# A decode step of sliding-window attention plus a gated MLP: the last chunk of w_down in 64 partitions, as eight loads of eight rows

## The chip, the core and the metric

The kernel runs on one core of a Trainium2 chip. A core has TensorE (PE, with its weight loads shown as PEld), VectorE (DVE), ScalarE (ACT), GpSimd (POOL) and SyncE (SP), which issues all the transfers of this kernel; 16 DMA engines carry them. Each engine runs its own list of instructions in order and waits on semaphores. The metric is the device time of one execution in microseconds (us); the time before is the median of three runs.

## The reference

One token for each of two batch rows goes through attention over the last 2048 positions of a cache and, beside it, through a bilinear gated MLP; both results are added to the input.

```python
xn = _layernorm(x, axis=-1)                       # x: [2, 1, 512]
q = (xn @ wq)                                     # 32 heads of 128
k, v = k_cache[:, :, Sk - W:], v_cache[:, :, Sk - W:]   # W = 2048
p = softmax(einsum("bhqd,bhkd->bhqk", q, k) * Dh ** -0.5)
attn = einsum("bhqk,bhkd->bhqd", p, v) @ wo
h = (xn @ w_gate) * (xn @ w_up)                   # F = 1376
out = x + attn + h @ w_down
```

Everything is float32. The two caches alone are 32 heads x 2 x 2048 x 128 values each, so nearly all of the 159 MB that the core reads is read once and used once.

## The kernel before

**Data.** The host lays all inputs out in one long array, `stream`, in the order of use. `blocks()` lists its pieces: for each piece a slot of SBUF, a first column and the fields in it. A field is a kind and an index: `k` and `vp` are a head's keys and values, `wo` and `wq` weights of the attention, `wg` and `wu` the gate and up weights, `wd` a chunk of 128 rows of w_down. Three slots (`step0` to `step2`) of 128 partitions x 15360 columns are used in turn; the small piece that comes first has a tile of its own, `first`, with the transposed input, two constant matrices and the query weights of the first two heads (`AHEAD` is 2, `DH` 128).

**The loads.** `pump()` takes the pieces in order and writes one load for each as soon as no live field lies in its columns; `done()` ends a field's life and calls `pump()` again. All loads go through SP's list, and so in order. The last piece is cut at row `LOW_ROWS` (88) into two loads of 88 and 40 rows.

**How waits come about.** `Flow.add` notes for each operation which operations it depends on: it compares the box of partitions and columns of each tile it touches with the boxes noted earlier. `Flow.box` gives a slice of partitions with a step as the whole stretch from its first to its last partition. `Flow.emit` turns a dependency into a semaphore wait where the two operations have different keys; each load is a key of its own, and any other operation has its engine as key:

```python
p1 = p0 + ps // row * (pn - 1) + 1
if (write or w) and a0 < p1 and p0 < a1 and b0 < f1 and f0 < b1:
    deps.add((m, w))
key = ("dma", n) if make[0] == "dma_start" else unit
```

The first line is from `box`; the next two are from `add` (`w` and `write` say whether the earlier and the later access write); the last is from `emit`.

**The work.** For each head DVE multiplies the keys by the query (`products`) and sums the products (`sums`), POOL and ACT make the softmax, PE multiplies by the values (`weigh`) and, for a group of heads, by `wo`. `gate()` makes the hidden vector of the MLP and transposes it in pieces of 128 into `hT` (and its last 96 values into `hX`); `down(c)` multiplies chunk c of w_down by it. There are ten whole chunks (`NFC` is 10). Chunks 0 and 1 and the rest rows are used early, chunk 2 (`HOLE`) late, and chunks 3 to 9 at the very end. All add up in one PSUM tile, `acc`; near the end each result is spread over four groups of 32 partitions, so that a chunk takes four products with 128 columns each (`accumulate`). In the trace a product in float32 is two matmul records. Chunk 8 comes in two halves by columns (`wh`): one with chunk 7, one with chunk 9 in the last piece. Behind chunk 9 DVE adds the input (`o_out`), and SP stores the result.

Of the kernel before, what the change touches and what calls it, by code (L numbers as in the profile page):

```python
# [15 lines left out]
P = 128  # L16
B, D, H, DH, SK, F = 2, 512, 32, 128, 8192, 1376
# [3 lines left out]
NC = D // P  # L21
FB = 4 * P
NFB = -(-F // FB)
NFC = F // P
FR = F - NFC * P
FH = [(0, 2 * FB), (2 * FB, F)]
RB = 8
M = RB * (B - 1) + 1
# [7 lines left out]
AHEAD = H + 1 - G * T  # L36
GC = G * DH
CQ = NC * GC
FIRST = AHEAD * DH
# [4 lines left out]
NE = 2  # L44
HOLE = NE
TAIL = list(range(NE + 1, NE + 5))
LOW_ROWS = 88
STEP = 30 * FB
BUFS = 3
BASE = 30 * 1024  # L50
# [10 lines left out]
def pitch(fields):  # L61

    n = -(-sum(w for _, _, w in fields) // BLK)
    return (n | 1) * BLK


def blocks():

    def k(*heads):
        return [("k", h, CK) for h in heads]

    def vp(h, p0=0, p1=NV):
        return [("vp", (h, p0, p1), FB * (p1 - p0))] + ([("wo", h, CO)] if p1 == NV else [])  # L80

    def wd(chunks):
        return [("wd", c, D) for c in chunks]

    def wh(c, half):
        return [("wh", (c, half), D // 2)]

    gu = [
        (kind, half, NC * (FH[half][1] - FH[half][0])) for half in range(2) for kind in ("wg", "wu")
    ]  # L90
    ones = [("pick", 0, 4 * SIDES * B), ("rows", 0, NFB * B)]
    out = [(None, 0, [("x", 0, B * NC)] + ones + [("w", 0, NC * FIRST)])]
    out.append((1, 0, k(*range(2)) + [("wq", 0, CQ)] + k(*range(2, AHEAD))))
    out.append((2, 0, gu + [("wr", 0, NS * P)] + wd(range(NE))))
    k0, v0 = AHEAD, 0
    for t in range(T - 1):
        a = vp(v0) + vp(v0 + 1, 0, VA)
        b = vp(v0 + 1, VA) + vp(v0 + 2, 0, VB)
        c = vp(v0 + 2, VB) + vp(v0 + 3) + vp(v0 + 4)
        out.append((0, 0, k(k0, k0 + 1) + a))  # L100
        out.append((1, 0, k(k0 + 2, k0 + 3) + [("wq", t + 1, CQ)] + b))
        out.append((2, 0, k(k0 + 4) + c))
        k0, v0 = k0 + G, v0 + G

    def put(slot, at, *groups):
        for fields in groups:
            out.append((slot, at, fields))
            at += sum(w for _, _, w in fields)
        return at

    put(0, 0, k(k0, k0 + 1), vp(v0) + vp(v0 + 1, 0, VA))
    at = put(1, 0, k(k0 + 2) + vp(v0 + 1, VA))
    put(1, at, vp(v0 + 2), k(k0 + 3))
    at = put(2, 0, vp(v0 + 3, 0, VA), vp(v0 + 3, VA), vp(v0 + 4))
    v30, v31 = vp(v0 + 5), vp(v0 + 6)
    put(2, at, v30[:1])
    c = NFC - 2
    put(
        0, 0, v31[:1], v30[1:] + v31[1:] + wd(TAIL[:1]), wd(TAIL[1:]), wd([c - 1]) + wh(c, 0),
        wh(c, 1) + wd([c + 1]),  # L120
    )
    return out


class Flow:
# [296 lines left out]
def sliding_attention_plus_glu_kernel(  # L422
# [6 lines left out]
    flow = Flow(nc)  # L429
    pe, dve, act, pl, sp = (flow.engine(unit) for unit in ("pe", "dve", "act", "pl", "sp"))  # L430
# [6 lines left out]
    first = None  # L437


    todo, at = [], 0  # L440
# [3 lines left out]
    got, live = {}, {}  # L444

    def pump():
        nonlocal first
        while todo:
            slot, c0, fields, at = todo[0]
            c1 = c0 + sum(w for _, _, w in fields)  # L450
            if any(s == slot and a < c1 and c0 < b for s, a, b in live.values()):
                return
            todo.pop(0)
            if slot is None:
                tile = first = flow.tile([P, c1], "first")
            else:
                tile = slots[slot]
            a = c0
            for kind, i, w in fields:
                got[kind, i] = tile[:, a : a + w]  # L460
                if slot is not None:
                    live[kind, i] = (slot, a, a + w)
                a += w
            src = stream[at : at + P * pitch(fields)].rearrange("(p i) -> p i", p=P)
            rows = [0, P] if todo else [0, LOW_ROWS, P]
            for p0, p1 in zip(rows, rows[1:]):
                sp.dma_start(tile[p0:p1, c0:c1], src[p0:p1, : c1 - c0])

    def done(kind, i):
        got.pop((kind, i))  # L470
        live.pop((kind, i), None)
        pump()
# [4 lines left out]
    rows = got["rows", 0]  # L477
# [39 lines left out]
    tr = flow.bank([P, 4 * P], "tr")  # L517
# [20 lines left out]
    xnb = flow.tile([P, NC * B, PB], "xnb")  # L538
# [3 lines left out]
    xnb = xnb.rearrange("p (c b) n -> p c (b n)", b=B)  # L542
# [3 lines left out]
    q_first = tr[:, P : P + FIRST]  # L546
    q_use = flow.bank([P, 2 * FB], "q_use")

    def project_first():
        w = got["w", 0].rearrange("p (c n) -> p c n", c=NC)  # L550
        for c in range(NC):
            pe.matmul(q_first, xnb[:, c, :], w[:, c, :], start=(c == 0), stop=(c == NC - 1))
        got.pop(("w", 0))

    def project_q(t):
        w = got["wq", t].rearrange("p (c n) -> p c n", c=NC)
# [65 lines left out]
    def columns(t):  # L622
        return [t[:, c : c + P] for c in range(0, t.shape[1], P)]

    def accumulate(lhsT, rhs, last=False):
        nonlocal n_acc
        for g in range(4):
            pe.matmul(
                acc_g[32 * g : 32 * g + M, :], lhsT, rhs[g],
                start=(n_acc == 0), stop=last,  # L630
            )
        n_acc += 1
# [54 lines left out]
    hT = flow.tile([P, 4, NFB, M], "hT")  # L687
    dve.memset(hT, 0.0)

    hX = flow.tile([P, NS, M], "hX")  # L690
    dve.memset(hX, 0.0)

# [14 lines left out]
    def gate():  # L707
        g_sb = flow.ring([P, FB], "o_sb", 2)
        act.copy(g_sb, gu_ps[0])
        h_sb = flow.ring([P, FB], "o_sb", 2)  # L710
        dve.tensor_tensor(h_sb, g_sb, gu_ps[1], op=ALU.mult)
        for i in range(4):
            t = tr[:, P + i * P // 2 : P + i * P // 2 + NFB * B]
            pe.matmul(t, h_sb[:, i * P : (i + 1) * P], rows, start=True, stop=True)
            act.copy(hT[:, i, :, ::RB], t.rearrange("p (n b) -> p n b", b=B))
        for i in range(NS):
            t = tr[:, P + (2 * i + 1) * P // 4 : P + (2 * i + 1) * P // 4 + NFB * B]
            f = (NFC % 4) * P + i * FX - FR
            pe.matmul(t, h_sb[:, f : f + P], rows, start=True, stop=True)
            act.copy(hX[FR:, i, ::RB], t[FR:, (NFB - 1) * B :])  # L720

    def down(c):
        lhsT = hT[:, c % 4, c // 4, :]
        if c == HOLE:
            w = got["wq", T - 1].rearrange("p (c n) -> p c n", c=NC)[:, :, GC - DH :]
            pe.matmul(acc, lhsT, w, start=False, stop=False)
            done("wq", T - 1)
        elif c < NE:
            pe.matmul(acc, lhsT, got["wd", c], start=(c == 0), stop=False)
            done("wd", c)  # L730
        else:
            fields = [("wd", c)] if ("wd", c) in got else [("wh", (c, half)) for half in range(2)]
            accumulate(lhsT, sum([columns(got[f]) for f in fields], []), last=(c == NFC - 1))
            for f in fields:
                done(*f)

    def down_rest():
        wr = got["wr", 0]
# [77 lines left out]
    for t in range(T - 1):  # L816
        h = AHEAD + G * t
# [7 lines left out]
    h = H - 4  # L825
    v = G * (T - 1)
    spare, o_ps2 = q_ps[:, :FB], q_ps[:, FB:]
    pair, tile = [v, v + 1], o_ps[0]
# [17 lines left out]
    pair, tile = [v + 2, v + 3], o_ps[1]  # L846
# [24 lines left out]
    for n in (v + 4, v + 5):  # L871
        tile = o_ps[n % 2]
# [14 lines left out]
    n = v + 6  # L887
# [3 lines left out]
    for k, t in enumerate((o_ps[n % 2], o_ps2)):  # L891
        for j in range(NV):
            kk, i = divmod(j, 4)
# [22 lines left out]
def laid_out(x):  # L916
# [4 lines left out]
    first = {  # L921
        kind: np.zeros((P, w), a.dtype) for kind, _, w in blocks()[0][2][:3]
    }
# [13 lines left out]
    wq = x["A_wq"].reshape(P, NC, H * DH)  # L937
# [5 lines left out]
    wd = x["B_w_down"]  # L943
    rest = wd[NFC * P :].reshape(FR, NS + 1, P)

    def field(kind, i):
        if kind in first:
            return first[kind]
        if kind == "k":
            return cache["k"][i]  # L950
        if kind == "vp":
            h, p0, p1 = i
            return cache["v"][h][:, FB * p0 : FB * p1]
        if kind == "w":
            return wq[:, :, :FIRST].reshape(P, -1)
        if kind == "wq":
            h = AHEAD + G * i
            w = wq[:, :, h * DH : (h + G) * DH]
            if i == T - 1:
                hole = wd[HOLE * P : (HOLE + 1) * P].reshape(P, NC, DH)  # L960
                w = np.concatenate([w, hole], axis=2)
            return w.reshape(P, -1)
        if kind == "wo":
            return wo[i]
        if kind == "wr":
            last = rest[:, NS, :].reshape(NS, FX, P).swapaxes(0, 1)
            return np.concatenate([rest[:, :NS, :], last]).reshape(P, NS * P)
        if kind == "wd":
            return wd[i * P : (i + 1) * P]
        if kind == "wh":  # L970
            c, half = i
            return wd[c * P : (c + 1) * P, half * (D // 2) : (half + 1) * (D // 2)]
        return gu[kind][:, :, FH[i][0] : FH[i][1]].reshape(P, -1)

    def part(fields):
# [42 lines left out]
```

## Time and profile before

| | us |
|---|---|
| median of three runs (377.70 to 377.87) | 377.84 |
| the profiled execution, its own time | 377.76 |
| span of its instructions | 376.4 |
| DVE busy | 302.8 |
| PE busy | 213.5 |
| ACT busy | 60.3 |
| POOL busy | 25.7 |

The core's queue of loads moved 159.54 MB in 4807 packets. In the profile all instructions that the helper `Flow` writes stand under one line, L350, so they are told apart by the names of their tiles. A row of the timeline gives the start, the duration, the engine, the operation with what it writes and reads, and in brackets how long the engine sat idle before it and what ended that; "SPq" is the time in which SP issues a transfer, not the transfer. Times of the trace are counted from the start of the span.

### The profile page before, as it was taken

The numbers are of one execution on the slowest core, as the hardware profiler recorded it, in microseconds if no ns is written. First come the engines' busy times: TensorE is split into PE (matmuls) and PEld (weight loads), VectorE is DVE, ScalarE is ACT, GpSimd is POOL, SyncE is SP. The second block draws the span as 40 slices with busy tenths as digits, with TensorE's granted clock in tenths as the row PEclk, the third lists the DMA queues.
The fourth block names the chain that finished last, engine by engine and source line by source line (L and its number), as shares of the span: only waits on it lengthen the run. The fifth ranks groups of instructions, "written<-read, shape, count | busy, mean of one in ns | idle before, by whom it ended". The sixth has DMA issues, their size and how long they took to land. (4 is left out here: it accounts for less than half of the span.)

```text
span 376.4 us, 2737 instructions
## 1 busy us (share of the span) xinstructions
PE 213.5 (57%) x990; PEld 75.5 (20%) x990; DVE 302.8 (80%) x182; ACT 60.3 (16%) x251; POOL 25.7 (7%) x84
## 2 busy tenths in 40 slices
PE   0552957385733285831395650596450677484796
PEld 0321223022200032200131210231110232021243
DVE  2159959999929999839999569999389999999920
ACT  1003120121311121301111301211201212211220
POOL 1000000000000000000000000000000000000000
PEclk9958786959878568968578967588976598889799
DMA  9999999999999999999999999999999999999995
GB/s 384 410 439 442 413 419 444 464 431 437 418 418 424 477 431 444 418 418 418 437 464 431 444 418 418 424 477 431 444 418 418 418 428 429 441 422 421 441 414 177
DMA packets 4813, 159.63 MB, mean 424 GB/s; under 512 B 567, under 2 KB 711, under 8 KB 1351
## 3 DMA queue, kind: packets, MB, share of 16 engines
q1 hardware_dynamic: 4807, 159.54, 98.4%
q8 instruction: 4, 0.07, 0.1%
q14 instruction: 2, 0.02, 0.0%
HBM read 159.48 MB, written 0.07 MB: 424 GB/s over the span
## 5 line engine op out<-in xcount | busy, mean ns | idle before, releaser
L350 PE MATMUL o_ps<-step,p 128*16 128x512 f32 (+3 forms) x512 | 101.3, 797 | 114.7 <-PEq L342 101.9
L350 DVE TENSOR_TENSOR step<-step,q_use 128x4096 f32<-128x4096 f32 x29 | 127.7, 4404 | 32.5 <-DMA step<-in_stream_dram 32.5
L350 DVE TENSOR_REDUCE s<-step 128x32 f32<-128x4096 f32 x32 | 141.4, 4420 | 1.1
L350 PEld LDWEIGHTS o_ps<-step,p 128*16 128x16 f32 (+2 forms) x512 | 21.0, 120 | 180.4 <-issue 161.7
L350 ACT ACTIVATE nm<-mm 128x2 f32<-128x2 f32 x32 | 6.5, 203 | 237.0 <-POOL mm L350 237.0
L350 PE MATMUL acc<-step,oT 128*9 128x512 f32 (+1 forms) x82 | 36.5, 609 | 7.0 <-PEq L342 6.0
L350 PE MATMUL q<-step,xnb 128*128 128x512 f32 (+1 forms) x96 | 30.5, 475 | 6.7 <-PEq L342 6.7
L350 POOL PARTITION_ALL_REDUCE mm<-m x32 | 11.3, 354 | 293.8 <-DVE m L350 293.8
L350 PE MATMUL tr<-first,o_sb 128*128 128x4 f32 (+2 forms) x134 | 23.2, 292 | 13.8 <-PEq L342 13.8
L350 PEld LDWEIGHTS tr<-first,o_sb 128*128 128x128 f32 x134 | 22.3, 244 | 29.8 <-issue 28.1
L350 DVE TENSOR_TENSOR step<-step,tr 128x4096 f32<-128x4096 f32 x3 | 13.2, 4414 | 11.2 <-DMA step<-in_stream_dram 11.2
L350 PEld LDWEIGHTS q<-step,xnb 128*128 128x128 f32 x96 | 16.3, 207 | 24.6 <-issue 24.6
L350 ACT ACTIVATE p<-s,nm 64x32 f32<-64x32 f32 x64 | 20.4, 319 | 1.4
L350 PE MATMUL o_ps<-step,xn 128*2 128x512 f32 (+1 forms) x48 | 12.5, 660 | 7.1 <-PEq L342 7.1
L350 POOL PARTITION_ALL_REDUCE sum<-rs x32 | 12.8, 399 | 39.5 <-ACT p L350 39.5
L350 ACT ACTIVATE oT<-tr,rec 128x1 f32<-128x1 f32 x58 | 10.1, 265 | 18.6 <-PE tr L350 18.6
L350 DVE TENSOR_REDUCE m<-s 64x1 f32<-64x32 f32 x64 | 11.5, 180 | 1.5
L350 ACT COPY o_sb<-o_ps 128x512 f32<-128x512 f32 (+1 forms) x16 | 9.1, 572 | 21.9 <-PE o_ps L350 21.8
L350 ACT ACTIVATION_READ_ACCUMULATOR p<-s,nm 64x1 f32 x64 | 11.8, 185 | 0.0
L350 PEld LDWEIGHTS acc<-step,oT 128*9 128x9 f32 x82 | 5.5, 96 | 24.0 <-issue 21.2
L350 DVE TENSOR_TENSOR oT<-tr,rec 128x2 f32<-128x2 f32 x3 | 0.5, 162 | 10.8 <-PE tr L350 10.8
L350 PE MATMUL acc<-step,hT 128*9 128x128 f32 (+2 forms) x64 | 7.5, 337 | 1.0 <-DMA step<-in_stream_dram 1.0
(47 smaller groups left out, 47.6 us busy)
## 6 DMA issues: line engine op xcount, KB each, us to landing
step<-in_stream_dram SPq DMA_DIRECT2D x15, 7680.0 KB, 35.4
step<-in_stream_dram SPq DMA_DIRECT2D x1, 7424.0 KB, 21.8
step<-in_stream_dram SPq DMA_DIRECT2D x1, 6208.0 KB, 36.0
step<-in_stream_dram SPq DMA_DIRECT2D x3, 2048.0 KB, 34.9
step<-in_stream_dram SPq DMA_DIRECT2D x2, 2304.0 KB, 24.1
step<-in_stream_dram SPq DMA_DIRECT2D x1, 4096.0 KB, 27.6
step<-in_stream_dram SPq DMA_DIRECT2D x1, 3584.0 KB, 28.9
step<-in_stream_dram SPq DMA_DIRECT2D x1, 3072.0 KB, 24.9
```

Source lines behind the costliest of these rows:

```text
L350: made = getattr(eng, method)(*args, **kwargs)
```

## The change

The 64 low and the 64 high rows of chunk 9 now lie side by side in 64 partitions, 1024 columns wide (a field of the new kind `wl`; the stream holds zeros for the other 64 partitions, and these are not loaded). This field is the last piece. It comes as eight loads: for each half of 32 partitions, four loads of eight rows, each with a step of four partitions, so that row number e of each load lies in partition p0 + 4e. Chunks 7 and 8 come whole in the piece before. Chunk 9 then takes eight products over 64 partitions where it took four over 128: four with the low half of its piece of `hT`, four with the high half, which `gate()` transposes once more into a new tile `hL`, at partitions 0 to 63. DVE clears `hL` once. The first piece of the stream becomes two: the input, the constants and the weights of one query head (550 columns), then the weights of the other head (1024 columns), both in the tile `first`.

```diff
-    def wh(c, half):
-        return [("wh", (c, half), D // 2)]
...
-    out = [(None, 0, [("x", 0, B * NC)] + ones + [("w", 0, NC * FIRST)])]
+    fields = [("x", 0, B * NC)] + ones + [("w", 0, NC * DH)]
+    out = [(None, 0, fields)]
+    out.append((None, sum(w for _, _, w in fields), [("w", 1, NC * (FIRST - DH))]))
...
-        0, 0, v31[:1], v30[1:] + v31[1:] + wd(TAIL[:1]), wd(TAIL[1:]), wd([c - 1]) + wh(c, 0),
-        wh(c, 1) + wd([c + 1]),
+        0, 0, v31[:1], v30[1:] + v31[1:] + wd(TAIL[:1]), wd(TAIL[1:]), wd([c - 2, c - 1]),
+        [("wl", c, 2 * D)],
...
-            src = stream[at : at + P * pitch(fields)].rearrange("(p i) -> p i", p=P)
-            rows = [0, P] if todo else [0, LOW_ROWS, P]
-            for p0, p1 in zip(rows, rows[1:]):
-                sp.dma_start(tile[p0:p1, c0:c1], src[p0:p1, : c1 - c0])
+            src = stream[at : at + P * pitch(fields)].rearrange("(p i) -> p i", p=P)[:, : c1 - c0]
+            if fields[0][0] == "wl":
+                for half in range(0, HALF, HALF // 2):
+                    for p0 in range(half, half + 4):
+                        rows = slice(p0, half + HALF // 2, 4)
+                        sp.dma_start(tile[rows, c0:c1], src[rows])
+            else:
+                sp.dma_start(tile[:, c0:c1], src)
...
+    hL = flow.tile([P, M], "hL")
+    dve.memset(hL, 0.0)
...
+        c = NFC - 1
+        t = tr[:HALF, P + 7 * P // 4 : P + 7 * P // 4 + NFB * B]
+        f = c % 4 * P + HALF
+        pe.matmul(t, h_sb[:, f : f + HALF], rows, start=True, stop=True)
+        act.copy(hL[:HALF, ::RB], t[:, c // 4 * B : (c // 4 + 1) * B])
...
+        elif c == NFC - 1:
+            w = columns(got["wl", c][:HALF])
+            accumulate(lhsT[:HALF], w[:4])
+            accumulate(hL[:HALF], w[4:], last=True)
+            done("wl", c)
         else:
-            fields = [("wd", c)] if ("wd", c) in got else [("wh", (c, half)) for half in range(2)]
-            accumulate(lhsT, sum([columns(got[f]) for f in fields], []), last=(c == NFC - 1))
-            for f in fields:
-                done(*f)
+            accumulate(lhsT, columns(got["wd", c]))
+            done("wd", c)
```

The two places where lists of instructions change most are SP's and PE's ends. The rows below name a load by its target and its shape (partitions x columns); `step_49` is slot 0. A name like `done_dma823` is the semaphore of one load. SP's list before, from the load that ends the values of the last heads on:

```order
L350 DMA step_49<-in_stream_dram 128x1536 [waits done_dve]
L350 DMA step_49<-in_stream_dram 128x1536
L350 DMA step_49<-in_stream_dram 128x768
L350 DMA step_49<-in_stream_dram 88x768 [waits done_pe]
L350 DMA step_49<-in_stream_dram 40x768
L350 DMA out_dram<-o_out 128x128 [waits done_dve]
```

The 88 and the 40 rows are the last piece; the second of the two is issued without a wait. SP's list with the change, the same place:

```order
L352 DMA step_49<-in_stream_dram 128x1536 [waits done_dve]
L352 DMA step_49<-in_stream_dram 128x1536
L352 DMA step_49<-in_stream_dram 128x1024
L352 DMA step_49<-in_stream_dram 8x1024 [waits done_pe]
L352 DMA step_49<-in_stream_dram 8x1024 [waits done_dma823]
L352 DMA step_49<-in_stream_dram 8x1024 [waits done_dma824]
L352 DMA step_49<-in_stream_dram 8x1024 [waits done_dma825]
L352 DMA step_49<-in_stream_dram 8x1024
L352 DMA step_49<-in_stream_dram 8x1024 [waits done_dma827]
L352 DMA step_49<-in_stream_dram 8x1024 [waits done_dma828]
L352 DMA step_49<-in_stream_dram 8x1024 [waits done_dma829]
L352 DMA out_dram<-o_out 128x128 [waits done_dve]
```

The eight loads have the semaphores `done_dma823` to `done_dma830`, in order. The second, third and fourth and the sixth, seventh and eighth each stand behind a wait for the load just ahead of them; the fifth has none of its own. PE's list before, from the first chunk of TAIL behind the last head on (`hT` are hidden values, `oT` a head's output):

```order
L350 MATMUL acc<-step_49,hT 9x128 [waits done_dma817]
L350 MATMUL acc<-step_49,hT 9x128 x11
L350 MATMUL acc<-step_49,oT 9x128 [waits done_dve]
L350 MATMUL acc<-step_49,oT 9x128 x3
L350 MATMUL acc<-step_49,hT 9x128 [waits done_dma818]
L350 MATMUL acc<-step_49,hT 9x128 x5
L350 MATMUL acc<-step_49,hT 9x128 [waits done_dma819,done_dma820]
L350 MATMUL acc<-step_49,hT 9x128 x5
```

Six products stand behind the wait for the last piece. PE's list with the change:

```order
L352 MATMUL acc<-step_49,hT 9x128 [waits done_dma821]
L352 MATMUL acc<-step_49,hT 9x128 x11
L352 MATMUL acc<-step_49,oT 9x128 [waits done_dve]
L352 MATMUL acc<-step_49,oT 9x128 x3
L352 MATMUL acc<-step_49,hT 9x128 [waits done_dma822]
L352 MATMUL acc<-step_49,hT 9x128 x7
L352 MATMUL acc<-step_49,hT 9x128 [waits done_dma826,done_dma830]
L352 MATMUL acc<-step_49,hT 9x128 x3
L352 MATMUL acc<-step_49,hL 9x128 x4
```

Eight products now stand behind the last piece, and their one wait is for the fourth and the eighth of the eight loads.

More of the change, by code (lines that the diff above doesn't have):

```diff
@@ L46 @@
 TAIL = list(range(NE + 1, NE + 5))
-LOW_ROWS = 88
+HALF = P // 2
 STEP = 30 * FB
@@ L116, in blocks @@
     put(2, at, v30[:1])
-    c = NFC - 2
+    c = NFC - 1
     put(
-        0, 0, v31[:1], v30[1:] + v31[1:] + wd(TAIL[:1]), wd(TAIL[1:]), wd([c - 1]) + wh(c, 0),
-        wh(c, 1) + wd([c + 1]),
+        0, 0, v31[:1], v30[1:] + v31[1:] + wd(TAIL[:1]), wd(TAIL[1:]), wd([c - 2, c - 1]),
+        [("wl", c, 2 * D)],
     )
     return out
+PRELUDE = sum(w for slot, _, fields in blocks() if slot is None for _, _, w in fields)
 class Flow:
@@ L454, in pump @@
             if slot is None:
-                tile = first = flow.tile([P, c1], "first")
+                first = first or flow.tile([P, PRELUDE], "first")
+                tile = first
             else:
@@ L549, in project_first @@
     def project_first():
-        w = got["w", 0].rearrange("p (c n) -> p c n", c=NC)
+        w = first[:, PRELUDE - NC * FIRST :].rearrange("p (h c n) -> p h c n", h=AHEAD, c=NC)
         for c in range(NC):
-            pe.matmul(q_first, xnb[:, c, :], w[:, c, :], start=(c == 0), stop=(c == NC - 1))
-        got.pop(("w", 0))
+            pe.matmul(
+                q_first.rearrange("p (h n) -> p h n", h=AHEAD), xnb[:, c, :], w[:, :, c, :],
+                start=(c == 0), stop=(c == NC - 1),
+            )
+        for n in range(2):
+            got.pop(("w", n))
     def project_q(t):
@@ L715, in gate @@
             act.copy(hT[:, i, :, ::RB], t.rearrange("p (n b) -> p n b", b=B))
+        c = NFC - 1
+        t = tr[:HALF, P + 7 * P // 4 : P + 7 * P // 4 + NFB * B]
+        f = c % 4 * P + HALF
+        pe.matmul(t, h_sb[:, f : f + HALF], rows, start=True, stop=True)
+        act.copy(hL[:HALF, ::RB], t[:, c // 4 * B : (c // 4 + 1) * B])
         for i in range(NS):
@@ L954, in field @@
         if kind == "w":
-            return wq[:, :, :FIRST].reshape(P, -1)
+            heads = slice(0, 1) if i == 0 else slice(1, AHEAD)
+            w = wq.reshape(P, NC, H, DH)[:, :, heads]
+            return w.transpose(0, 2, 1, 3).reshape(P, -1)
         if kind == "wq":
@@ L969, in field @@
             return wd[i * P : (i + 1) * P]
-        if kind == "wh":
-            c, half = i
-            return wd[c * P : (c + 1) * P, half * (D // 2) : (half + 1) * (D // 2)]
+        if kind == "wl":
+            w = wd[i * P : (i + 1) * P].reshape(2, HALF, D).swapaxes(0, 1).reshape(HALF, -1)
+            return np.concatenate([w, np.zeros_like(w)])
         return gu[kind][:, :, FH[i][0] : FH[i][1]].reshape(P, -1)
```

## The prediction

> **What bounds the kernel now.** First the page's slices, its row on the queue and its chain.
>
> ```profile
> DVE  2159959999929999839999569999389999999920
> DMA  9999999999999999999999999999999999999995
> q1 hardware_dynamic: 4807, 159.54, 98.4%
> HBM read 159.48 MB, written 0.07 MB: 424 GB/s over the span
> DVE 17%; DMA 16%; PE 1%; issue 0%; SPq 0%
> ```
>
> The 16 DMA engines are at nine tenths or more in all slices but the last; no other engine is. DVE comes near it in the middle but has slices at 3 and 2 where it waits for loads. So the time is that of the stream of loads, and what follows the last load. The chain of waits, read from its end, says the same:
>
> ```profile
> 339.54 0.33 SPq L350
> 339.91 32.29 DMA step<-in_stream_dram
> 372.20 0.04 issue
> 372.25 2.23 PE acc L350 x56
> 374.47 0.02 issue
> 374.49 0.29 DVE o_out L350
> ```
>
> The piece that ends late was issued at 339.54 us and landed 32 us later, as it stood behind the stream that had been issued before it. Loads that are issued early thus cost only their bytes. The timeline shows the end in detail:
>
> ```profile
> 343.92 2.18 SPq L350 DMA_DIRECT2D step<-in_stream_dram  x1
> 372.25 0.84 PE L350 MATMUL acc<-step,hT 128*9 128x128 f32 x24 [1.03 <-DMA step<-in_stream_dram]
> 373.27 1.17 PE L350 MATMUL acc<-step,hT 128*9 128x128 f32 x24
> 373.83 0.32 PEld L350 LDWEIGHTS acc<-step,hT 128*9 128x9 f32 x12 [0.24 <-DMA step<-in_stream_dram]
> 374.49 0.29 DVE L350 TENSOR_TENSOR o_out<-acc,x_nat 128x128 f32<-128x128 f32 x1 [3.08 <-PE acc L350]
> 374.81 0.37 SPq L350 DMA_DIRECT2D out_dram<-o_out  x1
> ```
>
> SP had issued the last piece by some 346 us. It landed just ahead of 373.83, where PE starts its last 12 records (six products); these end at 373.27 + 1.17 = 374.44. DVE and the store follow. So the last landing sets the end, at 373.8, and 376.4 - 373.8 = 2.6 us follow it.
>
> **The change part by part.** *The eight loads.* Only the first is issued early: it waits for a product of PE, as the 88-row load did, and goes out from about 344 us on. SP's list in the part on the change shows that the second, third, fourth, sixth, seventh and eighth each wait until the load ahead has landed. The boxes explain it: rows p0, p0+4, ... p0+28 count as one stretch of 29 partitions, so the four loads of a half overlap by the kernel's own bookkeeping though they write different rows. The fifth (partitions 32 on) has no wait, but stands behind the fourth in SP's list. So the loads no longer queue up 25 us ahead; six round trips stand one behind the other: second, third, fourth with the fifth just behind it, sixth, seventh, eighth. Only the wait of SP is new on the path; behind it in SP's list there is only the store, which had to come last anyhow, and PE's last eight products wait for the eighth load.
>
> What one round trip costs, no row shows for a small load in an empty queue. The nearest rows are the store, which meets an empty queue, and the first load of the program:
>
> ```profile
> first<-in_stream_dram SPq DMA_DIRECT2D x1, 787.0 KB, 4.5
> out_dram<-o_out SPq DMA_DIRECT2D x1, 64.0 KB, 1.6
> 7.41 0.54 SPq L350 DMA_DIRECT2D carry<-in_carry_dram  x1
> ```
>
> The store takes 1.6 us from issue to landing. The first load takes 4.5 us, of which 787 KB at 424 GB/s are 1.9, so 2.6 us without its data. A load of 32 KB lies between: 1.4 (a little below the store, which moves twice the bytes) to 2.3 us (below the 2.6, as that one met a program just starting). I take 1.6, by the nearer row, plus 0.03 for SP to see the landing, as the store starts at 374.81 and DVE ended at 374.78. Six trips are 6 x 1.63 = 9.8 us. The fifth load goes out after the fourth has been issued, which took 0.54 us for the small load `carry`; the sixth waits for the fifth, so 0.5 us is added: 10.3 us from the landing of the first load to that of the eighth (6 x 1.43 + 0.5 = 9.1 to 6 x 2.33 + 0.5 = 14.5 at the bounds).
>
> When the first small load lands: the stream holds the same bytes up to the end (128 x 1536 columns before, 128 x 1024 and 64 x 1024 now). In the old tail these ended at 373.8. Seven of eight rows of an engine are not yet issued, 7 x 4 KB; an engine moves 424 / 16 = 26.5 GB/s, so that is 1.1 us less: 372.7. Against this, the end of the stream ran far below its rate:
>
> ```profile
> 368.00:370.00 2.00, 2.00 (x48) 1.15 (x41) 0.00 (x0) 0.51 (x2) 0.00 (x0) 1.00 1.03 413
> 370.00:372.00 2.00, 1.22 (x18) 0.97 (x8) 0.16 (x1) 0.23 (x1) 0.00 (x0) 1.00 0.64 140
> 372.00:374.00 2.00, 1.75 (x52) 1.25 (x54) 0.00 (x0) 0.00 (x0) 0.00 (x0) 1.00 0.10 36
> ```
>
> (The last two columns of this view by stretches are the engines' busy share and GB/s.) From 368 to 370 a busy engine moved 413 / 1.03 / 16 = 25 GB/s, from 370 to 372 only 140 / 0.64 / 16 = 13.7, while the loads of 88 and 40 rows ran. If that slowness came from these two loads, it is gone, and up to 1 us of the 2 us stretch with it. I take 372.0, with 371.3 and 372.7 as bounds. The eighth load then lands at 372.0 + 10.3 = 382.3, against 373.8: 8.5 us later.
>
> The Trainium skill, "DMA: Bandwidth & Descriptors", section "Anatomy of one DMA", speaks against small loads in a chain: each has a fixed cost of about 2.0 us on GpSimd's path, nearly all of it the confirmation that the last byte has landed. No run here shows that path; the store's 1.6 us agrees in kind. By 2.0 us the chain would be an estimated 6 x 2.03 + 0.5 = 12.7 us, and the time 2.4 us longer than my sum.
>
> *PE's end.* Behind the last landing stand eight products, 16 records, in place of 12. The 12 took from 373.83 to 374.44, 0.61 us or 0.05 each; 16 take 0.8. That adds 0.2 us. PE also stands idle for some 9 us ahead of them, and may run them at a lower clock; 329.08 shows 512-column products after a wait of 5 us, 357.58 some without one.
>
> ```profile
> 329.08 5.52 PE L350 MATMUL o_ps<-step,p 128*16 128x512 f32 x26 [4.98 <-DMA step<-in_stream_dram]
> 357.58 2.17 PE L350 MATMUL o_ps<-step,p 128*24 128x512 f32 x16
> ```
>
> That is 0.21 us each against 0.14, a factor of 1.6; at most 16 x 0.05 x 0.6 = 0.5 us more. I take 0.3 for PE in all (0.2 to 0.7). The products of chunks 7 and 8 hide in SP's round trips.
>
> *The first load as two.* SP issues one more load at the start:
>
> ```profile
> 0.72 0.39 SPq L350 DMA_DIRECT2D first<-in_stream_dram  x1
> 1.17 1.78 SPq L350 DMA_DIRECT2D step<-in_stream_dram  x3
> 8.52 0.15 DVE L350 TENSOR_REDUCE st<-first 128x2 f32<-128x8 f32 x1
> 11.76 4.70 PE L350 MATMUL tr<-first,xnb 128*128 128x384 f32 x8 [1.21 <-DVE xnb L350]
> 23.02 4.42 DVE L350 TENSOR_TENSOR step<-step,tr 128x4096 f32<-128x4096 f32 x1 [11.16 <-DMA step<-in_stream_dram]
> ```
>
> The issue that follows the first comes 0.45 us later, and the new first load (550 of 1574 columns, 275 KB) keeps the engines busy for 275 KB / 424 GB/s = 0.65 us: no gap. Nothing is gained either: the old first load landed by 0.72 + 4.5 = 5.2, its first reader starts at 8.52 behind DVE's own memsets, PE's query product at 11.76, and DVE's first long product waits for the next load until 23.02. I take 0 (0 to 0.5 if a gap opens, as a gap in this stream is never made up).
>
> *`hL`.* One memset on DVE, one transposing product and one copy on ACT:
>
> ```profile
> 11.78 0.08 DVE L350 MEMSET hX<- 128x27 f32 x1
> L350 ACT COPY hX<-tr 32x2 f32<-32x2 f32 x3 | 0.5, 154 | 2.2 <-PE tr L350 2.2
> L350 ACT ACTIVATE nm<-mm 128x2 f32<-128x2 f32 x32 | 6.5, 203 | 237.0 <-POOL mm L350 237.0
> ```
>
> 0.08 us of DVE lies in its 11.16 us of waiting ahead of 23.02; 0.15 us of ACT in its 237 us of waiting. Without that cover they would cost 0.3 us together. I take 0.
>
> *Sum:* 8.5 + 0.3 = 8.8 us on the profiled execution's 377.76: **386.6 us**. That execution lies 0.08 below the median, less than any term here. Bounds: trips at 1.4, first landing at 371.3 and PE at 0.2 give 371.3 + 9.1 - 373.8 + 0.2 = +6.8; trips at 2.3, 372.7, PE at 0.7 and a gap of 0.5 give 372.7 + 14.5 - 373.8 + 0.7 + 0.5 = +14.6.
>
> **The rivals.** *The round trips are dear.* If an empty queue makes a load pay what the first load paid, 2.6 us a trip, the chain is 6 x 2.63 + 0.5 = 16.3 us and the time 6.0 us above the forecast, 392.6. For it speaks that it is the only load that met empty queues; against it, that it is 787 KB at the program's start. 6 in 100.
>
> *The waits cost nothing and the end of the stream gets faster.* Should the loads be under way together after all (each wait met before SP reaches it), the eight loads are like two old ones, and the rows that now lie in every fourth partition do away with the slow stretch from 370 to 372. That mechanism alone decides from the point where a round trip costs under 0.1 us. The last piece would land up to 1 us earlier, PE's end would take 0.3 back: 377.76 - 1.0 + 0.3 = 377.1, faster by 0.2%. For it speaks the fall from 25 to 13.7 GB/s; against it SP's list, where the waits stand. 2 in 100 for faster, 2 in 100 for a gain and a loss that meet (377.8). [...]
>
> *The change does not do what it says on SP.* If the wait of one of the six loads falls away, the chain is shorter by a trip, 385.0; that lies within the range and counts with the forecast.
>
> **How the numbers follow.** The forecast's own case, trips of 1.4 to 2.3 us, has 90 in 100. Its bounds give 377.76 + 6.8 = 384.6 and 377.76 + 14.6 = 392.4; the upper one needs all terms at their ends at once, so I cut it to trips of 2.0 and a first landing at 372.4: 372.4 + 12.7 - 373.8 + 0.6 = +11.9, 389.7. The range is 384.2 to 390. A difference of 0.2%, 0.75 us, is about what a measurement of this kernel can tell from no change. Slower by more: 0.96; within: 0.02; faster: 0.02.
>
> **What would show it.** In the profile after: SP's own waits show six that end with a load of the last piece, 1.4 to 2.0 us each, from 372 on; the page's slices show DMA and all engines nearly idle in the last one; the chain ends in SP and DMA pieces that alternate; 16 records of PE start at about 382. The start up to 23 us is as before within 0.5 us. The prediction is wrong if the small loads land within 2 us of each other, or if a round trip lies outside 1.4 to 2.3 us.

## The result: 13 us slower, and the profile after

The changed kernel takes 390.91 us (median of four runs, 390.26 to 391.48) against 377.86 us. The ratio is 1.0343 with a 95% interval of 1.0323 to 1.0362, so it is 3.2 to 3.6% slower. The forecast was 386.6 us with a range of 384.2 to 390: the direction and the cause were right, the size was a third too small, and the time lies 0.9 us above the range.

The page of the changed kernel shows where the time lies. First its slices (DVE, then DMA and the rate), its queue and its chain by engine:

```profile
DVE  2059959999659999299998399994899999999000
DMA  9999999999999999999999999999999999999910
GB/s 365 396 425 432 475 424 418 467 416 416 442 454 410 423 467 423 423 467 416 416 442 454 410 423 467 423 423 467 416 416 448 416 416 434 431 425 436 413 39 17
DMA 19%; DVE 17%; SPq 1%; PE 1%; issue 0%
```

In the kernel before only the last slice was not full; now the last two are nearly empty, though the core moves the same bytes. The chain of waits from 339 us on:

```profile
342.34 29.94 DMA step<-in_stream_dram
372.28 0.02 issue
372.29 2.71 DMA step<-in_stream_dram
375.02 2.02 DMA step<-in_stream_dram
377.06 0.62 SPq L352
377.73 2.20 DMA step<-in_stream_dram
379.94 2.11 DMA step<-in_stream_dram
382.07 2.19 DMA step<-in_stream_dram
384.27 2.18 DMA step<-in_stream_dram
386.50 1.08 PE acc L352 x16
387.60 0.29 DVE o_out L352
```

The first piece of DMA is the small load that was issued early; it lands at 372.28. Then six round trips follow each other, each from SP's issue to the landing: those of the second, third, fifth, sixth, seventh and eighth load. Between the second trip and the third stands one issue of SP (the fourth load's, 0.62 us), since the fifth load goes out right behind the fourth. The eighth load lands at 386.45, and PE and DVE come behind it. SP's own waits name the six:

```profile
SPq L352 <- DMA step<-in_stream_dram: 36.4, 6, 28.3
SPq L352 <- DVE o_out L352: 3.0, 1, 3.0
```

The longest, 28.3 us, is for the first small load, with seven loads still to issue; the other five take 8.1 us together. In the kernel before SP had nothing left to issue but the store when it waited that long, so its wait cost nothing:

```profile
SPq L350 <- DVE o_out L350: 28.7, 1, 28.7
```

What the engines do meanwhile in the changed kernel, by stretches of 2 us (PE, PEld, DVE, ACT and POOL busy, the granted clock, the DMA engines' share and GB/s):

```profile
370.00:372.00 2.00, 2.00 (x51) 1.77 (x45) 0.16 (x1) 0.37 (x1) 0.00 (x0) 1.00 0.32 127
374.00:376.00 2.00, 0.00 (x0) 0.00 (x0) 0.00 (x0) 0.00 (x0) 0.00 (x0) 1.00 0.01 2
376.00:378.00 2.00, 0.00 (x0) 0.00 (x0) 0.00 (x0) 0.00 (x0) 0.00 (x0) 1.00 0.05 16
378.00:380.00 2.00, 0.00 (x0) 0.00 (x0) 0.00 (x0) 0.00 (x0) 0.00 (x0) 0.54 0.14 33
386.00:389.50 3.50, 1.04 (x16) 0.43 (x16) 0.29 (x1) 0.00 (x0) 0.00 (x0) 0.50 0.07 19
```

Nothing computes between 374 and 386 us, the DMA engines are busy for 1 to 14% of it, and PE's granted clock has fallen to one half when its last products come.

### The profile page after: what moved, and what is told of

It reads as the page before. It is cut to its first block, busy times and chain, and to the rows that moved or that the text cites. A ratio compares the mean times of both kernels' runs of the same rounds, so it can differ in the third digit from the quotient of the medians.

```text
span 389.5 us, 2768 instructions
## 1 busy us (share of the span) xinstructions
PE 219.8 (56%) x1000; PEld 77.0 (20%) x1000; DVE 302.8 (78%) x183; ACT 60.5 (16%) x252; POOL 25.7 (7%) x84
## 5 line engine op out<-in xcount | busy, mean ns | idle before, releaser
L352 PE MATMUL o_ps<-step,p 128*16 128x512 f32 (+3 forms) x512 | 107.1, 835 | 106.9 <-PEq L344 94.8
L352 PEld LDWEIGHTS o_ps<-step,p 128*16 128x16 f32 (+2 forms) x512 | 22.3, 123 | 177.6 <-issue 160.5
L352 PE MATMUL acc<-step,oT 128*9 128x512 f32 (+1 forms) x82 | 34.8, 587 | 7.0 <-PEq L344 5.9
L352 PE MATMUL tr<-first,o_sb 128*128 128x4 f32 (+3 forms) x136 | 22.8, 285 | 15.2 <-PEq L344 15.2
L352 PEld LDWEIGHTS tr<-first,o_sb 128*128 128x128 f32 (+1 forms) x136 | 21.8, 236 | 30.4 <-issue 29.1
L352 PE MATMUL acc<-step,hT 128*9 128x128 f32 (+3 forms) x64 | 8.4, 365 | 13.6 <-DMA step<-in_stream_dram 13.6
```

The source lines that it names most:

```text
L352: made = getattr(eng, method)(*args, **kwargs)
```

## The experiments

The theory is that the 13 us are six round trips in a row, brought about by the kernel's own bookkeeping, and that neither small loads nor the products over 64 partitions cost much in themselves. Its rivals are that they do.

**No waits.** The eight loads no longer count as overlapping one another:

```diff
+        if self.batch is not None:
+            deps = {(m, w) for m, w in deps if m not in self.batch}
+            self.batch.append(len(self.ops))
```

(`batch` is set by `pump()` around the eight loads.)

> The changed kernel, but its bookkeeping no longer counts the eight loads of the last piece as overlapping one another, so SP issues all eight without a wait; the bytes and products are the same. Theory (the time is lost in six round trips one behind the other): the eight loads queue up early behind the stream, the first lands at about 372.3 us as in the changed kernel, seven more rows of an engine follow at about 0.17 us each, so the last lands near 373.5, and eight products end at about 374.4, as in the kernel before: 377.4 to 378.2 us. Rival (small loads, eight engines or products over 64 partitions are dear in themselves): it stays above 384 us.

378.03 us, ratio 1.0002 (0.9993 to 1.0011). Its chain:

```profile
348.87 25.63 DMA step<-in_stream_dram
374.50 0.04 issue
374.55 0.67 PE acc L356 x16
```

The last of the eight loads is issued at 348.87 us, and it waits only for the stream ahead of it. So the waits alone make 12.9 us of the 13.1 us. What is left of the change (loads of eight rows, products over 64 partitions, `hL`, the first load as two) is as fast as the kernel before; it need not be free, as that kernel turns out below to lose 1.1 us by the cut of its own last piece. The last landing, 374.50, is 1.0 us later than I expected and 0.7 us later than in the kernel before.

**One load of 64 rows.**

```diff
-                for half in range(0, HALF, HALF // 2):
-                    for p0 in range(half, half + 4):
-                        rows = slice(p0, half + HALF // 2, 4)
-                        sp.dma_start(tile[rows, c0:c1], src[rows])
+                sp.dma_start(tile[:HALF, c0:c1], src[:HALF])
```

> The changed kernel, but the last piece comes as one load of 64 rows. Theory (round trips): one load has no chain, so the time is that of the kernel before within 0.3 us: 377.5 to 378.2 us. If it matters which engine writes which partitions (the other idea behind the slow stretch at the end of the kernel before), this load, whose rows lie differently among the engines, ends up to 1 us later than the eight loads without waits. Rival (products over 64 partitions are dear): above 384 us.

377.47 us, ratio 0.9993 (0.9982 to 1.0004): no chain, no loss. By the medians it is 0.6 us faster than the eight loads without waits, and its last landing is at 373.38 where theirs is at 374.50. So eight queued loads may cost a little more than one, though the intervals of the two ratios overlap; and the expected cost of its rows' place in partitions did not show in the time.

**Four loads of sixteen rows, in a chain.**

```diff
-                for half in range(0, HALF, HALF // 2):
-                    for p0 in range(half, half + 4):
-                        rows = slice(p0, half + HALF // 2, 4)
-                        sp.dma_start(tile[rows, c0:c1], src[rows])
+                for p0 in range(4):
+                    rows = slice(p0, HALF, 4)
+                    sp.dma_start(tile[rows, c0:c1], src[rows])
```

> The changed kernel, but the last piece comes as four loads of sixteen rows, a step of four partitions apart, each still waiting for the one ahead: three round trips in place of six and one issue. Theory A (a trip costs 2.15 us whatever the number of rows): the last load lands at 372.3 + 6.5 = 378.8, 7.7 us earlier than in the changed kernel: 383.2 us. Theory B (a trip is dear because a load of eight rows is slow to issue, 0.62 us against 0.36 for the store): trips of about 1.7 us, 382.0 us.

383.43 us, ratio 1.0148 (1.0133 to 1.0162), by theory A. Its chain has three trips:

```profile
372.48 2.26 DMA step<-in_stream_dram
374.75 2.11 DMA step<-in_stream_dram
376.88 2.08 DMA step<-in_stream_dram
379.01 1.08 PE acc L352 x16
```

A load of sixteen rows takes the same 2.1 us as one of eight, so the price is that of the trip and not of its number of rows.

**Two chains beside each other.**

```diff
-                for half in range(0, HALF, HALF // 2):
-                    for p0 in range(half, half + 4):
-                        rows = slice(p0, half + HALF // 2, 4)
+                for p0 in range(4):
+                    for half in range(0, HALF, HALF // 2):
+                        rows = slice(half + p0, half + HALF // 2, 4)
```

> The changed kernel with its eight loads in another order: low half, high half, low half, high half. There are still six waits for a load of the last piece, but in two chains that run beside each other, of three round trips each. Theory (serial trips): 372.3 + 3 x 2.15 + one issue of 0.65 = 379.4 in place of 386.5, so 383.8 us. Rival (each wait or each small load costs its 2 us, no matter how they are ordered): as the changed kernel, 390.9 us.

384.18 us, ratio 1.0167 (1.0153 to 1.0182). The same eight loads with the same overlaps, 6.7 us less than the changed kernel. The chain holds three trips in place of six (2.12, 2.12 and 2.10 us), behind one issue of SP: what counts is how many trips stand one behind the other.

**The first load as two, alone.** The kernel before with this one part of the change (the order of these weights in the stream and the product that reads them, not shown, go with it):

```diff
-    out = [(None, 0, [("x", 0, B * NC)] + ones + [("w", 0, NC * FIRST)])]
+    fields = [("x", 0, B * NC)] + ones + [("w", 0, NC * DH)]
+    out = [(None, 0, fields)]
+    out.append((None, sum(w for _, _, w in fields), [("w", 1, NC * (FIRST - DH))]))
```

> The kernel before with one part of the change alone: the first load comes as two. Theory (it neither costs nor gains, since DVE and PE start on it late and the stream has no gap): 377.84 within 0.4 us. Rival (the stream starts later and never makes it up): slower by 0.5 to 1.2 us.

378.04 us, ratio 1.0011 (1.0001 to 1.0020): 0.4 us slower by the ratio (0.15 by the medians), at the edge of what can be told. DVE's first long product, which waits for the third load, starts at 23.34 in place of 23.02:

```profile
23.34 4.42 DVE L355 TENSOR_TENSOR step<-step,tr 128x4096 f32<-128x4096 f32 x1 [12.47 <-DMA step<-in_stream_dram]
```

It gains nothing, and the third load lands a little late. In the changed kernel the same product starts later still, 1.26 us behind the kernel before:

```profile
24.28 4.42 DVE L352 TENSOR_TENSOR step<-step,tr 128x4096 f32<-128x4096 f32 x1 [13.57 <-DMA step<-in_stream_dram]
```

This does not last. DVE's next product that waits for a load starts at 57.07 us in the changed kernel and at 57.06 in the kernel before, and PE's product behind the load that lands near 349 us starts at 349.49 against 349.67. So the stream as a whole is not late.

**Where a trip's time comes from.** Three kernels keep the waits and change what is loaded. In the first, seven of the eight loads copy from SBUF:

```diff
-                        sp.dma_start(tile[rows, c0:c1], src[rows])
+                        s = src[rows] if p0 == 0 else slots[1][rows, : c1 - c0]
+                        sp.dma_start(tile[rows, c0:c1], s)
```

> The changed kernel, but seven of the eight loads (all but those of rows 0, 4, ... 28) copy the same number of bytes from slot 1 of SBUF, not from HBM, so part of chunk 9 is left out of the result. The waits are the same. Theory (a trip is 2.15 us and not the store's 1.6 because it reads HBM): trips of about 1.6 us, six trips and one issue 3.3 us shorter, 387.6 us. Rival (the trip costs the same whatever is read; the store is cheap for another reason): 390.9 us.

Its total, 420.01 us, says nothing: the copies read a part of slot 1 that DVE writes later, so DVE had to wait for them. The trips can be read from the chain all the same:

```profile
377.69 1.80 DMA step<-step
379.51 1.80 DMA step<-step
381.32 1.80 DMA step<-step
383.15 4.43 DVE step L352
```

1.80 us with SBUF as the source, against 2.11 to 2.20 in the last four trips of the changed kernel: with these rows, reading HBM costs 0.3 to 0.4 us of the trip, but not all that lies above 1.6.

In the second, short rows from HBM:

```diff
-                        sp.dma_start(tile[rows, c0:c1], src[rows])
+                        w = c1 - c0 if p0 == 0 else P
+                        sp.dma_start(tile[rows, c0 : c0 + w], src[rows, :w])
```

> The changed kernel, but all eight loads except the first and the fifth... in short: every load whose rows do not start at partition 0 fetches 128 of its 1024 columns (512 bytes a row, like the store), so most of chunk 9 is left out of the result. Theory (the trip is a fixed time, not bytes): 4096 bytes at 25 GB/s are 0.16 us and 512 bytes 0.02, so six trips are 0.8 us shorter at most, 390.0 us. Rival (the bytes are what a trip costs beyond the store's 1.6 us): 387.6 us.

(The kernel shortens seven loads, all but the very first; the fifth starts at partition 32 and is short too.) 388.55 us, between the two expectations. Its trips, without the fourth load's issue between the second and the third, and PE's end:

```profile
372.18 2.04 DMA step<-in_stream_dram
374.24 1.83 DMA step<-in_stream_dram
376.75 1.91 DMA step<-in_stream_dram
378.68 1.81 DMA step<-in_stream_dram
380.50 1.80 DMA step<-in_stream_dram
382.32 1.80 DMA step<-in_stream_dram
384.17 1.08 PE acc L352 x16
```

A short row from HBM takes the same 1.80 us as a long row from SBUF. So a trip is about 1.8 us, and 4096 bytes a row from HBM add 0.35. That is more than the 0.16 us that these bytes take at the stream's rate, and less than the rival needs. The stretches of one trip show where its time lies. Here are the time from SP's issue to the first bytes and the stretch in which they move (last two columns: the DMA engines' share and GB/s), first in the changed kernel, whose load lands at 384.26, then with short rows, landing at 382.30:

```profile
382.07:383.40 1.33, 0.00 (x0) 0.00 (x0) 0.00 (x0) 0.00 (x0) 0.00 (x0) 0.50 0.00 0
383.40:383.80 0.40, 0.00 (x0) 0.00 (x0) 0.00 (x0) 0.00 (x0) 0.00 (x0) 0.50 0.31 82
```

```profile
380.50:381.90 1.40, 0.00 (x0) 0.00 (x0) 0.00 (x0) 0.00 (x0) 0.00 (x0) 0.50 0.00 0
381.90:382.00 0.10, 0.00 (x0) 0.00 (x0) 0.00 (x0) 0.00 (x0) 0.00 (x0) 0.50 0.17 41
```

In both, more than half of the trip is over before a byte moves. Long rows make the bytes themselves and the time behind them longer: 0.40 and 0.46 us here, against 0.1 and 0.3.

In the third, sixteen short rows, made like the second from the kernel with four loads:

```diff
-                    sp.dma_start(tile[rows, c0:c1], src[rows])
+                    w = c1 - c0 if p0 == 0 else P
+                    sp.dma_start(tile[rows, c0 : c0 + w], src[rows, :w])
```

> Four loads of sixteen rows that wait for one another, where the second to fourth fetch 128 of the 1024 columns (512 bytes a row), so part of chunk 9 is left out. Theory (a trip is SP's issue plus a fixed 1.2 us plus about 0.35 us for rows of 4096 bytes from HBM): SP's issue of sixteen rows is 0.49 us, so a trip is 1.7 us, against 2.1 with whole rows and 1.82 with eight short rows. Rival (the issue is no part of the trip, which is 1.82 us for any short load): 1.82 us.

382.31 us, and the trips are by the rival, 1.81 to 1.84 us:

```profile
372.36 1.83 DMA step<-in_stream_dram
374.21 1.81 DMA step<-in_stream_dram
376.04 1.84 DMA step<-in_stream_dram
```

So SP's shorter issue does not shorten the trip. Why the store lands after 1.6 us and a short load after 1.8 stays open.

**The slow end of the stream.** The prediction saw that a busy DMA engine moved 13.7 GB/s from 370 us on. First, the kernel before with its last piece as one load of 128 rows:

```diff
-            rows = [0, P] if todo else [0, LOW_ROWS, P]
+            rows = [0, P]
```

> The kernel before, but its last piece comes as one load of 128 rows, not as 88 and 40. Theory (the slow stretch at the end comes from loads whose rows lie across the engines' own partitions): from 370 us on a busy DMA engine keeps about 25 GB/s, where it had 13.7 in the kernel before, and the last landing is between 1 us earlier and the same, as three late engines now carry a full share: 377.0 to 378.0 us. Rival (the end of the stream is slow for another reason): 14 GB/s for a busy engine again, and a later end, 378 to 379 us.

376.74 us, ratio 0.9970 (0.9959 to 0.9981): faster than both kernels, and 0.3 us below the expected range. The stretches of this kernel and its last landing:

```profile
370.00:372.00 2.00, 2.00 (x52) 1.77 (x44) 0.16 (x1) 0.37 (x1) 0.00 (x0) 1.00 0.39 157
372.00:374.00 2.00, 1.38 (x44) 0.90 (x32) 0.29 (x1) 0.00 (x0) 0.00 (x0) 1.00 0.05 14
```

```profile
372.77 0.32 PEld L350 LDWEIGHTS acc<-step,hT 128*9 128x9 f32 x12 [0.17 <-DMA step<-in_stream_dram]
```

A busy engine moves 157 / 0.39 / 16 = 25 GB/s, the full rate, and the last landing is at 372.77 in place of 373.83. The expectation speaks of three late engines; no view names the engines, so that part is not shown. And the last landing no longer sets the end: PE is busy from 366 us to its last product without a pause, and the chain that ended last is PE's own up to DVE:

```profile
371.47 1.93 PE acc L350 x56
```

So the kernel before pays 1.1 us for the cut of its last piece, and against this better kernel the eight loads without waits are about 1.2 us slow (ratios 1.0002 and 0.9970). How firm is the 13.7 GB/s? The kernel with the first load as two ends in the same two loads of 88 and 40 rows, and its stretch gives 183 / 0.61 / 16 = 18.8:

```profile
370.00:372.00 2.00, 1.68 (x39) 1.46 (x39) 0.16 (x1) 0.00 (x0) 0.00 (x0) 1.00 0.61 183
```

Two executions with the same last loads thus differ by 5 GB/s, though both are below 25. Then eight loads without waits whose rows lie next to each other:

```diff
-                for half in range(0, HALF, HALF // 2):
-                    for p0 in range(half, half + 4):
-                        rows = slice(p0, half + HALF // 2, 4)
-                        sp.dma_start(tile[rows, c0:c1], src[rows])
+                for p0 in range(0, HALF, 8):
+                    rows = slice(p0, p0 + 8)
+                    sp.dma_start(tile[rows, c0:c1], src[rows])
```

> The changed kernel, but each of its eight loads takes eight rows that lie next to each other (0 to 7, 8 to 15, ...); these do not overlap in the bookkeeping, so none waits. It differs from the eight loads without waits (378.03 us) only in which partitions the loads write at a time. Theory (the slow stretch comes from several DMA engines that write into the same few partitions): a busy DMA engine falls well below 20 GB/s from 370 us on, where it kept 24.5, and the time is 0.5 to 3 us above that of the loads without waits: 378.5 to 381 us. Rival (which partitions are written does not matter): 24 to 25 GB/s and 378.0 within 0.5 us.

378.50 us, ratio 1.0015 (1.0007 to 1.0024), which fits both expectations. The same stretch here, in the kernel with one load of 64 rows, and in the one with eight loads without waits, in this order:

```profile
370.00:372.00 2.00, 2.00 (x48) 1.67 (x40) 0.16 (x1) 0.37 (x1) 0.00 (x0) 1.00 0.54 190
```

```profile
370.00:372.00 2.00, 2.00 (x52) 1.77 (x44) 0.16 (x1) 0.37 (x1) 0.00 (x0) 1.00 0.62 186
```

```profile
370.00:372.00 2.00, 1.79 (x36) 1.49 (x35) 0.16 (x1) 0.37 (x1) 0.00 (x0) 1.00 0.41 161
```

By the same division these are 22, 19 and 24.5 GB/s. The loads of all 128 rows and those with a step of four partitions keep the rate here; the other shapes fall below it, adjacent rows far less than I expected. Each figure is one execution, and the stretch holds bytes of the piece before as well, so 22 against 24.5 is not clear of a spread of 5. Nor does the rate order the ends: the load of 64 rows has the lowest rate and the earliest last landing, 373.38 against 374.05 with adjacent rows and 374.50 with steps. So that the place of the rows sets the rate, because several engines write into the same few partitions, was argued and not shown.

At last two kernels: the load of 128 rows once more, and chunk 9 alone as the last load, which has this edit beside that of `rows`:

```diff
-        0, 0, v31[:1], v30[1:] + v31[1:] + wd(TAIL[:1]), wd(TAIL[1:]), wd([c - 1]) + wh(c, 0),
-        wh(c, 1) + wd([c + 1]),
+        0, 0, v31[:1], v30[1:] + v31[1:] + wd(TAIL[:1]), wd(TAIL[1:]), wd([c - 1, c]),
+        wd([c + 1]),
```

> The kernel before with its last piece as one load of 128 rows, once more and beside the two others on the same chip: 376.7 us within 0.2 if its gain is that of the load's shape, 377.8 if the first time was luck.

> The kernel before with its last two pieces cut otherwise: chunks 7 and 8 whole, then chunk 9 alone as one load of 128 rows and 512 columns. Against the one load of 128 x 768 (376.74 us) the last landing is the same, as the bytes are, and four products stand behind it, not six: 0.2 us less, 376.5 us. Rival (what follows the landing is hidden or the pieces' order matters): 376.7 us or more.

376.71 us, ratio 0.9964 (0.9951 to 0.9978), and 376.60 us, ratio 0.9962 (0.9948 to 0.9975). The gain of the whole load holds; chunk 9 alone is not to be told from it. Both beat the kernel before by 0.2 to 0.5%.

## Why the prediction was right in kind and wrong in size

**The chain of waits: right.** Six trips, one behind the other, with the fifth load behind the fourth's issue, stand in the chain as the working had them; without the waits the loss is gone, and with half as many trips in a row about half of it is.

**The price of a trip: the step that failed.** "I take 1.6, by the nearer row", the store's, plus 0.03 for SP. Measured: 2.02 to 2.71 us, on average 2.24 (13.41 us for the six pieces of the chain). The chain took 386.45 - 372.28 = 14.2 us in place of 10.3; this is 3.9 of the 4.3 us that the forecast lacks. A short load costs 1.8 us, not the store's 1.6, and whole rows from HBM add 0.35. The working set the lower bound below the store because the store moves twice the bytes; but loads of sixteen rows, twice the bytes too, took the same trip as those of eight. The first trip is longer than the others in the changed kernel (2.71) and with sixteen rows (2.26), but not in the two chains (2.12); the cause is open. The Trainium skill's 2.0 us ("DMA: Bandwidth & Descriptors", "Anatomy of one DMA"), which I set aside, is nearer to the trips here than the store is, though it is given for another path. The time is divided otherwise than on that path, where most of it is the confirmation behind the last byte: in the two trips shown, 1.3 to 1.4 us go by before the first byte and 0.3 to 0.5 behind the last.

**The range.** The bounds, 1.4 to 2.3 us, held the average of the six trips and five of them, but not the first, 2.71, which by the prediction's last sentence speaks against it. With these bounds the sum went up to 392.4. I then cut the upper end to trips of 2.0, as if all terms had to be at their ends for more. They did not: one common price stood six times in the sum, so its error was multiplied by six, and that one term alone reached 390.

**The first landing:** 372.28 against 372.0, 0.3 us. The slow stretch did go with the two old loads (127 / 0.32 / 16 = 25 GB/s), as the working had it, but not a whole microsecond of time with it; the stretch of the changed kernel holds mostly the 128 rows of the piece before.

**PE's end:** 0.47 us more (1.08 against 0.61), where 0.3 was taken, and the parts were the wrong way round. At full clock the 16 records take 0.67 us, as in the kernel without waits, so four more cost 0.06, not 0.2; the clock that had fallen to one half while PE waited cost 0.4, not 0.1.

**The first load as two:** taken as 0; 0.4 us (0.04 to 0.8) when alone, near the bound of 0.5. The start up to 23 us was to be as before within 0.5 us; DVE's first long product is 1.26 us late (24.28 against 23.02). That is made up by 57 us, so it is no part of the 13 us. **`hL`** did not show in the time, as was said.

The terms add up: PE starts its last products at 386.50 in place of 373.83, 12.67 us later, and takes 0.47 longer, 13.14 in all; the two profiled executions, 390.89 and 377.76, differ by 13.13.

**The rivals.** The dear trip at 2.6 us would have given 392.6, which is nearer to the result than the forecast is; it had 6 in 100. By that rival's own sum the changed kernel's smaller first load (275 KB, 3.0 us to its landing, of which 0.65 are its data) leaves 2.3 us, close to the 2.24 measured; that row was not to be had before. The gain from the rows' place, without the waits, would have been nil: 378.03 with the changed loads. It was to be had in another way, by one load of all 128 rows.

## What to carry to other kernels

When transfers are cut into many small ones, read the waits of the issuing engine before the bytes: a helper that tracks partitions as one stretch makes loads with a step depend on each other, and each such wait turns a queued load into a full round trip of about 2 us. A price that stands several times in a row in a sum needs its whole uncertainty, times its count, in the range. And the plain load over all partitions, in one piece, was the fastest end of this stream, with 768 or with 512 columns.

## What the runs showed of the hardware

- A small load in an empty queue takes about 1.8 us from SP's issue to its landing, with eight or sixteen rows of 512 bytes from HBM or with eight rows of 4096 bytes from SBUF; eight or sixteen rows of 4096 bytes from HBM take 2.0 to 2.3 us, and once 2.7. The first trip of the chain of short rows took 2.04. Of a trip, 1.3 to 1.4 us lie before the first byte in the two trips shown. The store of 64 KB takes 1.6 us.
- In single executions, from 370 to 372 us, a busy DMA engine moved 24.5 to 25 GB/s with loads of 128 rows or with eight queued loads of rows four partitions apart; 13.7 and 18.8 with loads of 88 and 40 rows, 19 with 64, and 22 with eight adjacent rows. In the chain, with one or two such loads under way, it moved 33 / 0.14 / 16 = 15 to 16 / 0.05 / 16 = 20.
- PE's granted clock was still 1.00 from 376 to 378 us, up to 5 us after PE's work had ended at 372.93, 0.54 in the next 2 us, and 0.50 when work came again at 386 us. These 5 us are no fixed time: in the kernel before, a pause that began at 324.11 had it at 0.50 from 326.5 on.
